# Two key tiles as one unit of seven block products, the last tile's quarters stored one by one, and a new written order

## The chip, the core and the metric

The kernel runs on one core of a Trainium2 chip. A core has five engines that run their own instruction streams: TensorE (PE in the profile) multiplies matrices, VectorE (DVE) and ScalarE (ACT) do elementwise work, GpSimd (POOL) does small elementwise work and issues DMAs, SyncE (SP) issues DMAs. The operands lie in the on-chip memory SBUF; matrix products arrive in PSUM, which has eight banks. The engines wait for each other and for DMAs by semaphores.

The metric is device time in microseconds (us) of one execution; the kernel before takes 203.65 us, median of 3 runs (203.56 to 203.76).

## The reference, cut to what matters

```python
xn = layernorm(A_x)                          # [2048, 640]
q, k, v = split(xn @ wqkv)                   # 32 heads of 20
pq, pk = phi(q), phi(k)                      # phi(t) = (t + 1 if t > 0 else exp(t)) + 1e-6
kv = sum over s of pk[s]^T v[s]              # per head, 20 x 20
z  = sum over s of pk[s]                     # per head, 20
o  = (pq @ kv) / (pq . z + 1e-6)
s  = o @ wo
g  = silu(relu(xn @ w1) @ w2)                # w1 [640, 1728], w2 [1728, 640]
out = A_x + s * g                            # [2048, 640], bfloat16
```

Nothing of it is cut in either kernel. The 2048 rows are 16 tiles of 128 tokens; the 640 columns are five chunks of 128, or two halves of 320.

## The kernel before, in words

The kernel computes G = xn^T pk in place of v and kv (the v weights are multiplied into G later), folds kv and wo into one matrix wf, and so needs only the products with wq, wk, w1, w2, wf and G.

**Block products.** Most large products are done with the seven-product scheme (Strassen's, in Winograd's form): a 2 x 2 block product takes seven block products for eight, at the price of sums of the operands on VectorE before it and of additions of results after it. One such set is called a unit. Its steps are s1, s5, s6, s2, s7, s3, s4, each a group of matmuls into one PSUM bank with what evacuates it. Of the five chunks of 128 in the inner dimension, four go into the scheme and the fifth is added by plain matmuls, so that a unit of width 512 has 2, 2, 2, 3, 3, 3, 3 matmuls in this order (`unit`, line 1164 on; its matmuls have line 1198, its copies on ScalarE line 1205, the additions on VectorE line 970, where the helper `tt` stands). The units are named by a letter and a number:

- a and b: hidden layer, relu(xn w1), tokens 0 to 1023 (a) and 1024 to 2047 (b). p and q: the query product, the same two halves of the tokens. m: the fifth column block of the query product with the last block of the hidden layer.
- g: G, eight matmuls of 320 columns per step. u: the product with w2, seven matmuls of 320 columns per step. o: the product with wf, steps of 2, 2, 2, 3, 3, 3, 3 matmuls of 320 columns.
- k: two key tiles, 8+i and 12+i, in one unit of 320 columns (`k_unit`). The kernel before has its code but does not use it.

**Other steps in the order.** n8 to n15 take the statistics of a token tile (for 9 to 15), normalise it on VectorE (line 649) and transpose it by a DMA on SyncE (line 698). H and Q are plain blocks of five 512-column matmuls, hh the narrow last hidden block. Ka9 and Kb9 are the two halves of the key product of tile 9, five 320-column matmuls each (line 709), with exp and relu on ScalarE (line 1482); the second half lets VectorE form pk (lines 735, 737). T0 and T1 are the sums of xn that the units of the two token halves need: five VectorE operations, of which T1's read the transposed tiles 8 to 15. SQ, SH1, SH2, SM, SK are the sums of weights for the units of q, h, m and k. y0 to y15 add pk tile by tile into two running sums for z, by accumulating DMAs that GpSimd issues (line 897), y0 to y7 into one and y8 to y15 into the other; each waits for the one before on its sum. zm merges the first sum into the second, zs splits the result into a high and a low part (lines 910, 970), zc makes the column z (line 916), dn the denominators (line 929). The two running sums lie in the hidden layer's buffer, in places that the units b4 and b5 write later; those writes wait until the sums are read. c0 and c1 are the last row block of G. GS and GT are sums for g, uT, uSa, uSb, oT, oS those for u and o. do, rc, dv store the reciprocals of the denominators, load them spread out, and multiply them into the queries. kv0, kv1 and W0 to W5 (lines 1595, 1621) make wf, the results going to their place by DMAs. xa, xb, xc load x tiles 10-11, 12-13, 14-15; wa and wb load parts of w1, w2a to w2d parts of w2; wo, wv0, wv1 the other weights; rb brings the row scales in by a transposing DMA; mv6 builds a small mask on GpSimd. e0, e1, e3 and f0, f1, f3 are halves of the last two token tiles, product with wf (e) and gating, addition of x and store (f); l0 and l1 are the two quarters of the last tile's first half (`s_last`), 160 columns each, five matmuls of 160 columns (line 1826).

**What sets the order.** The text PROGRAM (line 345) lists all steps after the head. TensorE and SyncE run exactly in this order. For ScalarE, VectorE and GpSimd a planner (`Sched.place`) orders the operations once, when the kernel is built, from estimated durations: it takes what can start first, and of several the one whose result is due first, among the next 60 operations. On the chip each engine runs its list in that order. The start of the kernel (layer norm of the first tiles, the key tiles 0 to 7, five hidden blocks) is written out before PROGRAM and is the head.

**The places of the key sums.** In the kernel before the sums of a k unit are laid out over the first running z sum and over wk itself:

```python
kSv = {i: two(regH[:, f * S + 1024:f * S + 1024 + 2 * HN], HN) for i, f in ((1, 4), (2, 10), (4, 3))}
kS3 = wk[:, 0:2, HN:D].bitcast(f16)
```

Of the kernel before, what the change touches and what calls it, by code (L numbers as in the profile page):

```python
# [346 lines left out]


def bass_recurrent_scan__linear_attn_block__dense_activation_relu__prompt_kernel(
# [135 lines left out]
    sumk = {9: [("hTs", 0, 5)], 5: [mSk[0], ("zacc", 1)], 11: [mSk[1], ("zacc", 1)], 4: [("zacc", 0)], 10: [("zacc", 0)]}  # L485
    hSk = [("hSs", u, i) for u in range(3) for i in (1, 2, 4)]
    NG = len(g_slots)
    mhalf = nc.alloc_sbuf_tensor("mhalf", [P, 1], f32)
# [416 lines left out]
        z_put(1, zacc[0], ("zacc", 0))  # L905

    def z_split():
        assert nz == [ZA, T + 1 - ZA - len(LATE)] and ("zacc", 1) not in dead, (nz, dead)
# [1 line left out]
        sc.op("ACT", lambda eng: eng.activation(out=hi, in_=zacc[1], func=ACTF.Copy), R=[("zacc", 1)],  # L910
              W=[("zhi",), ("ek_e", 0)])
# [737 lines left out]

    def gate_q(t, n, src, key):  # L1650
        g, sl = g_of(t)
        sc.op("ACT", lambda eng: eng.activation(out=g[:, HN * n:HN * (n + 1)], in_=src, func=ACTF.Silu),  # L1652
              R=[key, ("silu",)], W=[("g", sl, n)], extra=hz([("wv", 0), ("wv", 1)] + gtk))
# [296 lines left out]
```

## Time and profile before

| | |
|---|---|
| median of the runs | 203.65 us |
| profiled execution | 203.94 us |
| its span, first to last instruction | 202.7 us |
| TensorE busy | 198.6 us, 98% of the span, 1334 matmuls |
| VectorE busy | 172.2 us, 85% |
| ScalarE busy | 128.5 us, 63% |
| GpSimd busy | 37.2 us, 18% |
| granted TensorE clock | 1.000 |

A row of the groups reads: line, engine, operation, output <- inputs with shapes, count, then busy time and the mean of one in ns, then the engine's idle time before them and who ended it. A row of the timeline reads: start, duration, engine, line, operation, and in brackets the idle time just before it and what ended it; "xN" merges N neighbours. A row of the chain of waits reads: start, duration, what ran or was waited for. A row of the stretches reads: from:to, length, then busy time and instruction count of PE, weight loads, DVE, ACT and POOL, then clock, the DMA engines' share and GB/s. A row of waits reads: waiter <- releaser, total us, times, longest. Busy times count each engine's own overlaps once; matmul durations in the timeline are longer than the distance of their starts, since matmuls overlap.

### The profile page before, as it was taken

To read this page: it belongs to the slowest core of one execution; us is meant where nothing else is said; L and a number is where in the kernel's file an instruction comes from. 1 tells how busy PE (TensorE), PEld (TensorE's weight loads), DVE (VectorE), ACT (ScalarE), POOL (GpSimd) and SP (SyncE) were. 2 spreads that over 40 slices of the span, in tenths; PEclk is the share of its full clock that TensorE was granted. 3 is DMA by queue.
4 is the path that set the end of the run, shared out by engine and by line. 5 is a ranking of instruction groups with operands and counts; after the bars stand their busy time and mean duration, and the time that the engine had idled before them with its cause. 6 is when DMAs were issued, how large, how long until landed. Compare 5 with 4: busy or idle time off the path is not lost.

```text
span 202.7 us, 3677 instructions
## 1 busy us (share of the span) xinstructions
PE 198.6 (98%) x1334; PEld 123.8 (61%) x1344; DVE 172.2 (85%) x404; ACT 128.5 (63%) x268; POOL 37.2 (18%) x66
## 2 busy tenths in 40 slices
PE   8999999999999999999999999999999999999995
PEld 7755644545444454445645778777777777777773
DVE  4898999999997678899988879999978896855765
ACT  6497959799988486999662132463544645563452
POOL 3183051332256436422200000000000000000000
DMA  6976995662359858963462799338961106106103
GB/s 194 330 210 126 261 205 111 141 143 44 68 131 178 172 108 162 226 129 65 96 167 56 241 293 315 117 98 256 366 209 65 66 32 165 65 26 173 65 16 113
DMA packets 38328, 30.43 MB, mean 150 GB/s; under 512 B 13478, under 2 KB 38310, under 8 KB 38310
## 3 DMA queue, kind: packets, MB, share of 16 engines
q1 hardware_dynamic: 32437, 23.24, 41.0%
q0 software_dynamic: 4624, 5.57, 14.0%
q10 hardware_dynamic: 1248, 1.39, 2.1%
q8 instruction: 10, 0.16, 0.3%
q14 instruction: 9, 0.07, 0.1%
HBM read 15.81 MB, written 5.24 MB: 104 GB/s over the span
## 4 chain that ended last, share of the span: by engine, by line
PE 82%; DMA 11%; issue 3%; DVE 3%; ACT 0%; POOLq 0%; DVEq 0%
PE psT L1025 42%; PE psT L1198 18%; PE psT L709 10%; DMA regH<-reg 6%; PE psT L799 5%; DMA regH<-regH 3%; DMA reg<-in_A_x_dram 1%; PE psT L817 1%; PE psT L761 1%; PE psT L1826 1%; PE psT L682 1%; PE psT L1621 1%; PE psT L1595 1%; DVE regH L970 1%; PE psT L929 1%
## 5 line engine op out<-in xcount | busy, mean ns | idle before, releaser
L1198 PE MATMUL psT<-reg 128*128 128x512 bf16 (+1 forms) x135 | 36.8, 379 | 0.5 <-DVE regH L970 0.2
L1025 PE MATMUL psT<-reg,regH 128*128 128x320 bf16 (+1 forms) x224 | 35.0, 299 | 0.0
L1025 PE MATMUL psT<-reg 128*128 128x320 bf16 (+1 forms) x178 | 28.6, 299 | 0.0
L1025 PEld LDWEIGHTS psT<-reg,regH 128*128 128x128 bf16 (+1 forms) x224 | 21.9, 98 | 8.5
L1198 PEld LDWEIGHTS psT<-reg 128*128 128x128 bf16 (+1 forms) x141 | 13.4, 98 | 16.6 <-DVE regH L970 1.1
L897 POOL DMA_DIRECT2D regH<-reg x16 | 18.4, 1206 | 24.7 <-DMA regH<-reg 8.7
L1032 ACT ACTIVATE reg<-psT 128x320 f32<-128x320 f32 (+1 forms) x24 | 10.4, 435 | 17.8 <-PE psT L1025 15.9
L1025 PEld LDWEIGHTS psT<-reg 128*128 128x128 f16 (+1 forms) x178 | 17.4, 98 | 6.9
L970 DVE TENSOR_TENSOR reg<-reg 128x1024 f16<-128x1024 bf16 (+9 forms) x28 | 18.7, 673 | 1.1 <-PE psT L1025 1.0
L709 PE MATMUL psT<-reg 128*128 128x320 bf16 x120 | 18.7, 299 | 0.0
L1248 ACT ACTIVATE regH<-psT 128x512 bf16<-128x512 f32 (+1 forms) x24 | 15.2, 644 | 2.5 <-PE psT L1198 2.1
L1025 PE MATMUL psT<-reg,pqT 128*128 128x320 bf16 (+1 forms) x84 | 16.6, 299 | 0.0
L970 DVE TENSOR_TENSOR psT<-psT,reg 128x320 f32<-128x320 f32 (+1 forms) x21 | 11.4, 543 | 5.7 <-PE psT L1025 3.9
L1652 ACT ACTIVATE wv_sb<-psT 128x320 bf16<-128x320 f32 x22 | 9.6, 437 | 10.3 <-PE psT L1025 10.2
L709 PEld LDWEIGHTS psT<-reg 128*128 128x128 bf16 x120 | 11.7, 98 | 7.0
L1482 ACT ACTIVATE regE<-psT 128x320 bf16<-128x320 f32 x32 | 13.8, 538 | 2.9 <-PE psT L709 2.8
L630 DVE BATCH_NORM_STATS2 stats<-reg 128x6 f32<-128x320 bf16 x32 | 14.1, 473 | 1.3 <-DMA reg<-in_A_x_dram 1.3
L1032 ACT ACTIVATE psT<-psT 128x320 f32<-128x320 f32 x17 | 7.2, 426 | 10.3 <-PE psT L1025 10.3
L970 DVE TENSOR_TENSOR reg<-psT,reg 128x320 bf16<-128x320 f32 (+2 forms) x17 | 8.4, 499 | 4.2 <-PE psT L1025 4.1
L1841 ACT ACTIVATE reg<-psT 128x640 bf16<-128x640 f32 (+1 forms) x14 | 7.9, 569 | 5.1 <-PE psT L1025 5.1
L778 ACT ACTIVATE pqT<-psT 128x512 bf16<-128x512 f32 x16 | 10.6, 669 | 0.0
L776 ACT ACTIVATE regE<-psT 128x512 bf16<-128x512 f32 x16 | 10.1, 664 | 0.7 <-PE psT L761 0.5
(164 smaller groups left out, 385.5 us busy)
## 6 DMA issues: line engine op xcount, KB each, us to landing
regH<-reg POOLq DMA_DIRECT2D x16, 320.0 KB, 3.8
reg<-in_B_w_dram SPq DMA_DIRECT2D x12, 320.0 KB, 4.7
scr<-rden SPq DMA_DIRECT2D x4, 640.0 KB, 6.2
reg<-in_A_x_dram SPq DMA_DIRECT2D x4, 640.0 KB, 8.8
out_dram<-reg SPq DMA_DIRECT2D x14, 160.0 KB, 1.8
regE<-scr SPq DMA_DIRECT2D x3, 640.0 KB, 4.7
reg<-in_A_x_dram SPq DMA_DIRECT2D x4, 320.0 KB, 3.5
reg<-in_A_wo_dram SPq DMA_DIRECT2D x6, 160.0 KB, 5.2
```

The source lines that it names most:

```text
L630: sc.op("DVE", lambda eng: eng.bn_stats(stats[:, t, a, :], xv[:, HN * a:HN * (a + 1)]), R=[("xin", xs(t))], W=[("stats", t, a)])
L709: fns.append(lambda eng, a=a, k=k, lhs=lhs: eng.matmul(ps[bk[a]][:, 0:HN], lhsT=lhs, rhs=wk[:, k, HN * a:HN * (a + 1)], start=(k == 0), st ...
L776: exps.append(sc.op("ACT", lambda eng: eng.activation(out=e_, in_=src, func=ACTF.Exp), R=[key], W=[("er_e", es)]))
L778: sc.op("ACT", lambda eng: eng.activation(out=pqT[:, f, schunk(j)], in_=src, func=ACTF.Relu), R=[key], W=[("pqT", j, f)], extra=hz(gone))
L799: sc.group("PE", [(lambda eng, k=k: eng.matmul(ps[b], lhsT=w1_col(k, P * f, P), rhs=src[:, k, :], start=(k == 0), stop=(k == C - 1))) for ...
L897: dma("POOL", lambda eng: eng.dma_start(zacc[a], src, **kw), R=[key] + after, W=[("zacc", a)], chain=zchain[a])
L970: sc.op("DVE", lambda eng: eng.tensor_tensor(out=out, in0=in0, in1=in1, op=op), R=R, W=W, extra=extra)
L1025: sc.group("PE", [(lambda eng, k=k, lhs=lhs, rhs=rhs: eng.matmul(ps[b][:, 0:HN], lhsT=lhs, rhs=rhs, start=(start and k == 0), stop=(k == n ...
L1032: sc.op("ACT", lambda eng: eng.activation(out=dst, in_=ps[b][:, 0:HN], func=ACTF.Copy), R=[("ps", b)], W=[dkey], extra=extra)
L1198: sc.group("PE", [(lambda eng, k=k, lhs=lhs, rhs=rhs: eng.matmul(ps[b][:, 0:nn], lhsT=lhs if tile is None else rhs, rhs=rhs if tile is Non ...
L1248: sc.op("ACT", lambda eng: eng.activation(out=dst, in_=ps[b], func=ACTF.Relu), R=[("ps", b)], W=[("hT", j, f)], extra=ex)
L1482: sc.op("ACT", lambda eng, func=func, slot=slot: eng.activation(out=ek[:, eks(t), slot, HN * a:HN * (a + 1)], in_=ps[b][:, 0:HN], func=fun ...
```

## The change

1. The halves Ka9, Kb9, Ka13 and Kb13 leave the order; k1 (its seven steps) and SK come in. The sums of the k unit get other places, in the hidden layer's buffer at blocks 2, 3, 4 and 8, 9, 10, and the units b2, b3 and b4 wait to write there until k1 has read them. No sum lies over wk any longer.
2. The gate of the last tile's first half is done in two ScalarE operations of 160 columns. Each quarter is multiplied, added to x and stored by itself, l0's store on SyncE, l1's on ScalarE's queue; before, one addition and one store on ScalarE's queue served both.
3. The whole text PROGRAM is replaced by another order of the same other steps.

```diff
-xa T0 H14 SQ H112 n8 H15 H111 H110 xc n9 xb Q14 wb Q04 p1.s5 rb a1.s5 a1.s1 p1.s1 n11 Kb8 a1.s6 p1.s6 wa n10 p1.s2 SH1 a1.s2 a1.s7 n14 p1.s7 Ka9 a1.s3 a1.s4 n12 p1.s3 n15 p1.s4 p0.s1 Ka8 p0.s5 a0.s5 p0.s6 a0.s1 p0.s2 Kb11 a0.s6 p0.s7 p0.s3 n13 Ka10 Ka11 a0.s3 p0.s4 a0.s7 a0.s2 Kb9 Ka14 a3.s1 a0.s4 a2.s5 Kb12 a3.s5 a3.s6 a2.s1 hh0 hh1 y0 a2.s6 a3.s7 a2.s2 a3.s3 y1 a3.s2 a2.s7 a3.s4 T1 b1.s5
...
-q1.s6 y7 Kb15 m1.s1 y2 q1.s7 q1.s3 y6 m1.s5 q1.s4 y12 m1.s6 Ka15 m1.s2 m1.s7 b3.s1 b3.s5 m1.s3 b3.s6 w2a y13 m1.s4 b3.s2 b3.s3 SH2 b4.s1 b4.s5 y15 b3.s7 c0 b3.s4 c1 b5.s1 GT3 GS0 zm b4.s6 b5.s5 b4.s2 w2b b5.s6 b4.s7 zs GT1 b5.s2 w2d b4.s3 b4.s4 b5.s3 zc b5.s7 mv6 dn b5.s4 g0.s1
...
-g1.s4 uT3 uT2 do1 u0.s1 uSa0 kv1 kv0 u0.s5 u0.s6 sl W5
...
-e0 o6.s6 u7.s7 o6.s7 f0 o6.s3 e3 o6.s4 e1 u7.s3 u7.s4 l0 l1 f3 f1
+H111 H14 H15 xb H112 T0 H110 Q14 a0.s1 a0.s5 xa SQ n8 hh0 a0.s6 Q04 p1.s1 a0.s3 Kb8 rb a0.s7 p1.s5 a0.s2 p1.s6 a0.s4 p1.s2 a1.s5 a1.s1 n12 p1.s3 xc wa p1.s7 wb a1.s2 n11 a1.s6 Ka8 n13 SH1 p1.s4 SK a1.s3 n10 n15 p0.s5 mv6 n14 a1.s7 n9 p0.s1 Kb12 Ka12 a1.s4 p0.s6 a2.s5 a2.s1 p0.s2 p0.s3 a2.s6 p0.s7 a2.s2 T1 a2.s7 p0.s4 a2.s3 a2.s4 Kb11 b0.s1 k1.s1 k1.s5 Ka11 k1.s6 b0.s5 k1.s2 b0.s6 k1.s7 b0.s2 k1.s3 b0.s7 k1.s4 b0.s3
...
+Ka14 y2 y0 y14 b2.s7 y15 q1.s4 b2.s3 b2.s2 b2.s4 b3.s1 Ka10 GS0 GT1 GT2 b3.s5 w2a m1.s1 b3.s6 m1.s5 b3.s2 m1.s6 b3.s3 SH2 GT3 m1.s2 zm m1.s7 b3.s7 m1.s3 m1.s4 y10 zs b3.s4 c0 b4.s1 b5.s5 w2b b5.s1 w2d b4.s5 b4.s6 b4.s2 c1 b4.s7 b4.s3 b5.s6 b4.s4 g0.s5 g0.s1 b5.s3 b5.s2 b5.s7 zc g0.s6 b5.s4 g0.s2 dn g0.s3
...
+g1.s4 u0.s1 kv1 do1 kv0 W5 rc0 sl u0.s5
...
+uSb7 e1 u7.s7 o6.s4 e0 u7.s3 e3 f0 u7.s4 f1 f3 l0 l1
```

```diff
-    kSv = {i: two(regH[:, f * S + 1024:f * S + 1024 + 2 * HN], HN) for i, f in ((1, 4), (2, 10), (4, 3))}
-    kS3 = wk[:, 0:2, HN:D].bitcast(f16)
+    kSv = {i: regH[:, :].bitcast(f16).rearrange("p (f s) -> p f s", f=NK)[:, f:f + 7:6, o:o + HN]
+           for i, f, o in ((1, 4, 1024 + D), (2, 3, 1536), (4, 2, 1024), (3, 2, 1024 + HN))}
+    kS3 = kSv[3]
...
+    for i, f in ((1, 3), (2, 2)):
+        for f_ in (f, f + 6):
+            sumk[f_] = sumk.get(f_, []) + [kSk[i]] + [("kS3",)] * (f == 2)
...
-            tt(kS3, A11, A21, ALU.subtract, w, [("kS3",)], hz(w))
+            tt(kS3, A11, A21, ALU.subtract, w, [("kS3",)])
...
     def gate_q(t, n, src, key):
         g, sl = g_of(t)
-        sc.op("ACT", lambda eng: eng.activation(out=g[:, HN * n:HN * (n + 1)], in_=src, func=ACTF.Silu),
-              R=[key, ("silu",)], W=[("g", sl, n)], extra=hz([("wv", 0), ("wv", 1)] + gtk))
+        cuts = [(LC[i], LC[i + 1], ("g", sl, n) if i == 0 else ("glast",)) for i in range(2)] if t == LAST and not n else \
+            [(HN * n, HN * (n + 1), ("g", sl, n))]
+        for lo, hi, q in cuts:
+            sc.op("ACT", lambda eng, lo=lo, hi=hi: eng.activation(
+                out=g[:, lo:hi], in_=src[:, lo - HN * n:hi - HN * n], func=ACTF.Silu),
+                R=[key, ("silu",)], W=[q], extra=hz([("wv", 0), ("wv", 1)] + gtk))
...
-        tt(tmpo[:, NOUT, lo:hi], ps[b][:, 0:hi - lo], g[:, lo:hi], ALU.mult, [("ps", b), ("g", gslot[LAST], 0)],
-           [("tmpo", NOUT, 2 + i)])
-        if i:
-            s_store(LAST, NOUT, (2, 3), 0, HN, "DVE", "ACT")
+        tt(tmpo[:, NOUT, lo:hi], ps[b][:, 0:hi - lo], g[:, lo:hi], ALU.mult,
+           [("ps", b), ("glast",) if i else ("g", gslot[LAST], 0)], [("tmpo", NOUT, 2 + i)])
+        tt(outb[:, NOUT, lo:hi], tmpo[:, NOUT, lo:hi], xre[:, LAST, lo:hi], ALU.add,
+           [("tmpo", NOUT, 2 + i), ("xre", LAST // 4)], [("outb", NOUT, 2 + i)])
+        dma("ACT" if i else "SP", lambda eng: eng.dma_start(out2[tok(LAST), lo:hi], outb[:, NOUT, lo:hi]),
+            R=[("outb", NOUT, 2 + i)])
```

More of the change, by code (lines that the diff above doesn't have):

```diff
@@ new lines @@
+H111 H14 H15 xb H112 T0 H110 Q14 a0.s1 a0.s5 xa SQ n8 hh0 a0.s6 Q04 p1.s1 a0.s3 Kb8 rb a0.s7 p1.s5 a0.s2 p1.s6 a0.s4 p1.s2 a1.s5 a1.s1 n12 p1.s3 xc wa p1.s7 wb a1.s2 n11 a1.s6 Ka8 n13 SH1 p1.s4 SK a1.s3 n10 n15 p0.s5 mv6 n14 a1.s7 n9 p0.s1 Kb12 Ka12 a1.s4 p0.s6 a2.s5 a2.s1 p0.s2 p0.s3 a2.s6 p0.s7 a2.s2 T1 a2.s7 p0.s4 a2.s3 a2.s4 Kb11 b0.s1 k1.s1 k1.s5 Ka11 k1.s6 b0.s5 k1.s2 b0.s6 k1.s7 b0.s2 k1.s3 b0.s7 k1.s4 b0.s3 Kb14 a3.s5 a3.s1 b0.s4 Ka15 a3.s6 hh1 b1.s1 a3.s7 b1.s5 a3.s3 b1.s6 a3.s2 a3.s4 y8 b1.s2 q0.s5 q0.s1 b1.s7 Kb15 y12 y11 q0.s6 b1.s3 y7 b1.s4 q0.s2 ZS q0.s7 q0.s3 q1.s1 y9 y4 y3 y6 q0.s4 y1 q1.s5 q1.s6 b2.s5 Kb10 SM y5 b2.s1 q1.s2 y13 q1.s3 b2.s6 q1.s7 Ka14 y2 y0 y14 b2.s7 y15 q1.s4 b2.s3 b2.s2 b2.s4 b3.s1 Ka10 GS0 GT1 GT2 b3.s5 w2a m1.s1 b3.s6 m1.s5 b3.s2 m1.s6 b3.s3 SH2 GT3 m1.s2 zm m1.s7 b3.s7 m1.s3 m1.s4 y10 zs b3.s4 c0 b4.s1 b5.s5 w2b b5.s1 w2d b4.s5 b4.s6 b4.s2 c1 b4.s7 b4.s3 b5.s6 b4.s4 g0.s5 g0.s1 b5.s3 b5.s2 b5.s7 zc g0.s6 b5.s4 g0.s2 dn g0.s3 uSa0 g1.s1 GS1 w2c GT4 g0.s7 wo g1.s5 do0 g1.s6 g0.s4 uT3 wv0 g1.s7 g1.s2 uT1 g1.s3 uT2 wv1 g1.s4 u0.s1 kv1 do1 kv0 W5 rc0 sl u0.s5 W2 uSb0 W4 u0.s6 do2 uT4 u0.s2 W3 u0.s7 u0.s3 u2.s1 uSa2 W1 dv0 u2.s5 u0.s4 u2.s6 W0 uSa1 u2.s2 uSb2 rc1 u1.s1 uSa4 u1.s5 xre u1.s6 u1.s2 u2.s7 uSb1 u2.s3 oS0 uSb4 u1.s7 u1.s3 u2.s4 u1.s4 oT o0.s5 u4.s5 o0.s1 u4.s1 o0.s6 do3 o0.s2 u4.s6 o0.s3 o0.s7 rc2 u4.s7 o0.s4 uSa3 u4.s3 o1.s1 u4.s2 oS1 o1.s5 dv1 o1.s6 u4.s4 o1.s2 o1.s7 o2.s1 oS2 o2.s5 o1.s3 o1.s4 o2.s6 o2.s2 u3.s5 o2.s7 u3.s1 rc3 o2.s3 uSa6 uSb3 o2.s4 u3.s6 uSa5 o3.s1 oS3 u3.s2 o3.s5 o3.s6 u3.s7 dv2 u3.s3 oS4 o3.s7 o3.s2 u3.s4 u5.s5 u5.s1 uSb5 o3.s3 o3.s4 u5.s6 o4.s1 o4.s5 u5.s2 uSb6 o4.s6 u5.s7 u5.s3 oS5 o4.s2 o4.s7 u5.s4 o4.s3 o4.s4 u6.s1 o5.s1 o5.s5 u6.s5 uSa7 u6.s6 o5.s6 o5.s2 u6.s2 o5.s7 u6.s3 dv3 u6.s7 o5.s3 o5.s4 u6.s4 u7.s1 oS6 o6.s1 u7.s5 o6.s5 u7.s6 o6.s2 o6.s6 u7.s2 o6.s3 o6.s7 uSb7 e1 u7.s7 o6.s4 e0 u7.s3 e3 f0 u7.s4 f1 f3 l0 l1
@@ L907, in z_split @@
     def z_split():
-        assert nz == [ZA, T + 1 - ZA - len(LATE)] and ("zacc", 1) not in dead, (nz, dead)
+        assert nz == [ZA, T + 1 - ZA - len(LATE)] and ("zacc", 1) not in dead
         hi, lo = [v.rearrange("p (a n) -> p a n", a=2) for v in zhl]
@@ L1643, in bass_recurrent_scan__linear_attn_block__dense_activation_relu__prompt_kernel @@
     gslot = {}
+    LC = [0, 160, 320]
+    LAST = 15
     def g_of(t):
@@ L1806, in s_room @@
         return rooms[t]
-    LC = [0, 160, 320]
-    LAST = 15
     def s_mult(t, os_, i, lo, hi, src, keys, na):
```

3 lines of the change are left out of this document (1 added, 2 removed).

## The prediction

> **What bounds the kernel now.** I read the page first, then PE's waits, the chain of waits, and the timelines around the places that the new order moves.
>
> ```profile
> span 202.7 us, 3677 instructions
> ...
> PE 198.6 (98%) x1334; PEld 123.8 (61%) x1344; DVE 172.2 (85%) x404; ACT 128.5 (63%) x268; POOL 37.2 (18%) x66
> ...
> PE psT L1198 <- DVE regH L970: 0.2, 1, 0.2
> ...
> 49.77 1.36 PE psT L709 x10
> ...
> 41.04 2.37 PE psT L1198 x11
> ```
>
> TensorE (PE) is busy 98% of the span. Its list of waits holds, beside the start, one row, of 0.2 us. The chain's two rows give its pace: ten 320-column matmuls in 1.36 us are 0.136 us each, eleven 512-column ones in 2.37 us are 0.216. TensorE runs the written order as it stands, so I can place every step by counting matmuls from 23.30 us, where the order begins. Before the step b4.s4 stand 293 of 512 columns, 112 of 320 and the two hh steps (2.27 us in the chain): 104.05 by the count. The trace:
>
> ```profile
> 23.30 5.34 PE psT L799 x24
> ...
> 75.22 0.69 PE psT L709 x5
> ...
> 93.06 1.19 POOL L897 DMA_DIRECT2D regH<-reg  x1 [5.66 <-DVE regE L782]
> ...
> 97.48 1.19 POOL L897 DMA_DIRECT2D regH<-regH  x1 [3.23 <-DMA regH<-reg]
> ...
> 103.75 0.74 ACT L910 ACTIVATE regE<-regH 128x640 bf16<-128x640 f32 x1 [1.75 <-DMA regH<-regH]
> ...
> 103.82 0.69 DVE L970 TENSOR_TENSOR regH<-psT,wv_sb 128x512 bf16<-128x512 f32 x1 [0.62 <-PE psT L1198]
> ...
> 104.51 0.83 DVE L970 TENSOR_TENSOR regE<-regH,regE 128x640 bf16<-128x640 f32 x1
> ...
> 104.56 0.60 PE L1198 MATMUL psT<-reg 128*128 128x512 f16 x2 [0.18 <-DVE regH L970]
> ...
> 108.12 0.76 PE psT L1198 x3
> ...
> 134.50 0.27 PE psT L1621 x2
> ```
>
> Step Ka12 is counted to 75.18 and starts at 75.22: no time is lost until there. b4.s4 starts at 104.56, and W0 (count 133.69) at 134.50. So some 0.7 us are lost, nearly all between 100 and 109 us: 0.34 at b4.s4 (the matmul before it started at 104.00 and takes 0.216), 0.11 in the three matmuls at 108.12 (0.76 for 0.65), the rest in slivers at zc, b5.s7 and dn. The cause is in the rows: the merge of the two z sums (97.48) lands at about 103.72; only then may VectorE (DVE) write tile 10 of hT over the first sum (103.82), and only then is the PSUM bank free that b4.s4 wants.
>
> **Part 1: the unit.** Ka9, Kb9, Ka13 and Kb13 are 20 matmuls of 320 columns. k1 has 2+2+2+3+3+3+3 = 18. Gain 2 x 0.136 = **0.27 us** of TensorE. It costs, each at the nearest row:
>
> ```profile
> L970 DVE TENSOR_TENSOR reg<-reg 128x640 f16<-128x640 bf16 x3 | 1.4, 484 | 0.0
> ...
> L970 DVE TENSOR_TENSOR psT<-psT,reg 128x320 f32<-128x320 f32 x16 | 7.9, 496 | 4.1 <-PE psT L1025 3.9
> ...
> L1032 ACT ACTIVATE psT<-psT 128x320 f32<-128x320 f32 x17 | 7.2, 426 | 10.3 <-PE psT L1025 10.3
> ```
>
> VectorE: four weight sums (SK) at 0.48 and two additions from PSUM at 0.50, 2.9 us. ScalarE (ACT): two copies at 0.43, 0.86 us; exp and relu stay eight. Neither engine bounds the span, so this costs nothing where they have room. VectorE has none where it falls:
>
> ```profile
> 27.50:54.85 27.35, 27.19 (x148) 13.73 (x152) 26.64 (x76) 25.04 (x57) 6.71 (x17) 1.00 0.54 114
> ...
> 41.25 11.98 SPq L698 DMA_TRANSPOSE reg<-reg  x5
> ...
> 51.34 0.44 DVE L649 TENSOR_SCALAR reg<-reg,mv,rsy 128x640 bf16<-128x640 bf16 x1
> ...
> 54.88 0.68 DVE L970 TENSOR_TENSOR reg<-reg 128x1024 f16<-128x1024 bf16 x1
> ...
> 55.48 0.69 DVE L970 TENSOR_TENSOR psT<-psT,wv_sb 128x512 f32<-128x512 f32 x1
> ...
> 49.22 0.28 POOL L636 TENSOR_SCALAR rsv<-mv 128x1 f32<-128x1 f32 x1 [5.86 <-DVE mv L634]
> ...
> 54.90 1.69 POOL L897 DMA_DIRECT2D regH<-reg  x2 [3.80 <-DMA reg<-reg]
> ```
>
> In this stretch VectorE (fourth pair) works 26.64 of 27.35 us. The last of the tiles 8 to 15 is normalised at 51.34, its transpose is the last of the five at 41.25, and it lands at about 54.85: there T1, the five sums over these tiles, begins (54.88) and GpSimd (POOL) gets its first z sum. Before, their first reader was b1.s5, counted to 61.26: 6.4 us of room. After, b0.s1 (125 of 512, 25 of 320, one hh: 54.82) reads all eight tiles; k1.s5 (55.52) wants T1's first sum and SK's first; k1.s6 (56.47) three sums of T1 and two of SK. From T1's start that takes 3 x 0.60 (start to start: 54.88 to 55.48) + 2 x 0.41 (estimate: 0.48, less the 0.08 by which the sum of 54.88 overlaps the next) = 2.6 us. So TensorE waits unless T1 starts by 53.9, a microsecond sooner than now. Before T1 VectorE has two more evacuations (a2.s6, a2.s7, 0.6 each) and one K tile less (0.7): +0.5. It can put off what nobody awaits, four sums of p0 and one K tile, some 2 us; the new order asks for all norms by 45 us, so these go first. I take T1 at 54.1 and a wait of **0.2 us**. Ends: 0 (these sums put off) and 1.5 (T1 at 55.4, nothing put off). SyncE (SP) carries the same 7 transposes, 3 x loads, rb, wa and wb, in another order: xc, wa and wb now stand behind n12's transpose, so behind VectorE's norm of tile 12. SH1, which needs wa and wb, feeds a2.s5 at 47.66; with n12 at 35 us there are ten microseconds for it, so 0. mv6's six small POOL operations move from 106 to 44 us into POOL's waits for VectorE (5.86 us before the row at 49.22): 0; without that cover six at that row's 0.28, 1.7 us, on the norms' way.
>
> **Part 2: the z chain.** The last K half is Ka10 (86.2) for Ka15 (87.4), and zc moves from 105.3 to 107.9. The order on this chain is now y14, y15, merge, y10, split. By the rows a step takes 4.42 us (93.06 to 97.48), a merge 6.25 (to 103.73), a split 1.6. With y14 issued at X, the merge lands at X+15.1 and the split is done at X+21.1. b4.s4, counted to 103.13, can start if the merge lands by 102.4; zc if the split is done by 108.1. Both give X up to about 87.2.
>
> ```profile
> 61.50:80.00 18.50, 18.39 (x94) 9.12 (x94) 13.93 (x31) 13.38 (x28) 8.61 (x9) 1.00 0.77 150
> ...
> 80.00:97.00 17.00, 16.95 (x88) 8.46 (x88) 15.66 (x37) 16.93 (x36) 5.65 (x5) 1.00 0.63 139
> ...
> 91.24 0.88 ACT L1482 ACTIVATE regE<-psT 128x320 bf16<-128x320 f32 x2
> ...
> 92.28 0.48 DVE L737 TENSOR_TENSOR reg<-regE 128x640 bf16<-128x640 bf16 x1
> ```
>
> Ka14's matmuls end at 82.6 by the count. Before, Ka15's ended at 88.1 and its z sum went out at 93.06, 5.0 later: ScalarE evacuated it only at 91.24 and VectorE finished at 92.7. ScalarE (fifth pair) has room until 80 us and none from 80 to 97; Ka15 came 7.4 us into that full stretch. Ka14 comes at 81.9, and the q and m steps that fill ScalarE (ten and seven activations each) stand wider apart around it, so its backlog should be smaller. Without any, evacuation and finish take 0.88 + 0.9 us, about 1.8; with the old one 5.0. Nearer the old, since q1 still runs there, I take 4.2 us, X = 86.8, and the **0.55 us** of waits between 100 and 109 go. Ends: all 0.7 go; or 0.6 stay, with X = 87.6 or more.
>
> **Part 3: from 110 us on.** The same steps in another order. VectorE's reciprocals come 4.7 us later with dn (110.9); do0 then is behind wo on SyncE, and the divided q is first wanted at o0, 146 us: covered. The one spot with no cover is W5, which before stood two u steps after kv0 and now follows it at once:
>
> ```profile
> 125.04 1.44 PE psT L1595 x30
> ...
> 126.15 0.95 DVE L970 TENSOR_TENSOR reg<-psT,mv 128x40 bf16<-128x40 f32 x3
> ...
> 128.22 0.71 PE L1621 MATMUL psT<-reg 128*128 128x320 bf16 x4
> ```
>
> kv1's half of these matmuls (0.72 of 1.44) must be evacuated by two of the three DVE operations (0.6 together) while kv0's 0.72 run: a wait of 0 if VectorE is free, 0.6 if it is in a sum of 0.62. I take **0.2**.
>
> **Part 4: the tail.**
>
> ```profile
> 199.40 0.85 PE L1826 MATMUL psT<-reg,pqT 128*128 128x160 bf16 x10
> ...
> 199.60 0.44 ACT L1652 ACTIVATE wv_sb<-psT 128x320 bf16<-128x320 f32 x1 [0.51 <-PE psT L1025]
> ...
> 200.06 0.55 DVE L970 TENSOR_TENSOR reg<-psT,wv_sb 128x160 bf16<-128x160 f32 x2 [0.27 <-ACT wv_sb L1652]
> ...
> 200.65 0.33 DVE L1819 TENSOR_TENSOR reg<-reg 128x320 bf16<-128x320 bf16 x1
> ...
> 201.01 0.37 ACTq L1822 DMA_DIRECT2D out_dram<-reg  x1
> ...
> L1841 ACT ACTIVATE reg<-psT 128x640 bf16<-128x640 f32 x7 | 4.9, 701 | 4.4 <-PE psT L1025 4.4
> ...
> L1819 DVE TENSOR_TENSOR reg<-reg 128x640 bf16<-128x640 bf16 x14 | 6.7, 486 | 0.1
> ...
> out_dram<-reg ACTq DMA_DIRECT2D x1, 80.0 KB, 1.6
> ```
>
> From the gate's start to the last store's issue it is 1.41 us. After: first half gate 0.31 (estimate: 320 columns take 0.44, 640 take 0.70), product 0.32; second product about 0.67 to 0.99, when its matmuls too are done (200.25, 0.65 after the gate); sum of 160 columns 0.25 (estimate from 0.33 for 320 and 0.49 for 640): issue at 1.28 if VectorE takes both products first, 1.44 if sum 0 goes between. One store more, on SyncE, which has the f stores behind it. Gain **0.13**, ends 0.25 and -0.05.
>
> The rule against it: the Trainium skill ("DMA: Bandwidth & Descriptors", Specifications) puts 512 B as the least transfer for full rate, with a read-modify-write below. The quarters' rows are 320 B, the half's 640 B. By that rule the last store would land later, not sooner; the time is in the third rival.
>
> **Sum.** -0.27 - 0.55 - 0.13 + 0.2 + 0.2 = -0.55 us. The profiled execution took 203.94 us (span 202.7 and 1.2 around it), 0.29 above the median of 203.65. Against it the sum gives 203.4, against the median **203.1**.
>
> **The rivals.**
> 1. VectorE is late at 55 us (slower). For: 26.64 of 27.35 us are taken already, and 6.4 us of room become none. Against: some 2 us of it can wait. Each 0.1 us by which T1 starts after 53.9 is 0.1 us of TensorE; the sum without this wait is -0.75, so it decides for slower (over +0.4) from T1 at about 55.05, 0.2 later than now. With T1 at 55.4 to 56.2: 204.4 to 205.2.
> 2. The z chain is as late as before, pk14 5.0 us or more after Ka14. For: the merge and two steps more stand behind y14. Against: Ka14 meets ScalarE earlier in its full stretch. Then 0.6 us stay: 203.7.
> 3. The quarters don't shorten the tail, because their stores land later. For: a smaller store gains little, 1.6 us for 80 KB. Against: half the bytes. If the 40 KB land 0.2 us later than the 80 KB did, the tail gains nothing and loses 0.1: 203.3.
>
> **How the numbers follow.** 0.2%, 0.41 us, is about what a measurement of this kernel can tell from no change. My forecast (waits at 100 to 109 gone, little new) 0.47, all but a little of it below 203.24; rival 1 0.26; rival 2 0.20; rival 3 0.07. Faster 0.46, same 0.28, slower 0.26. The forecast's own range is 202.6 (no new wait, every old one gone) to 203.3. The range reaches into rival 1 as far as 204.5: below and above it I leave 0.2.
>
> **What would show it.** The K halves' matmuls fall by 20, and the units' line gains 18 of 320 columns. Around 55 us: the start of T1 (the first 1024-column f16 sum after the last transpose) and any gap before k1.s6. At 100 to 109: the regH<-regH merge against b4.s4. At 125: the gap before the first L1621. At the end: two 160-column sums and two 40 KB stores, issue to span end. The prediction is wrong if T1 starts after 55, or if a stretch that I called covered (SyncE's order at 30 to 45 us, the reciprocals at 112 to 117) shows waits of TensorE.

## The result and the profile after

The kernel after takes 203.28 us (median; 202.88 to 203.87), the kernel before 203.81 us beside it (203.41 to 204.16). The ratio is 0.9973 with a 95% interval of 0.9965 to 0.9980: 0.55 us less, between 0.41 and 0.71. The forecast was 0.55 less and 203.1 us. The total came out, but most of its terms did not, and they made up for each other; that the total is so close is luck. The profiled execution of after took 202.95 us, its span is 201.7 us. Lines of the kernel text stand four further down than before up to about line 1640 and eight or nine behind that: the units' matmuls are on L1202 for L1198, those of g, u and o on L1029 for L1025, the sums on L974 for L970.

The head of the page of after:

```profile
span 201.7 us, 3704 instructions
...
PE 198.4 (98%) x1342; PEld 122.7 (61%) x1342; DVE 172.9 (86%) x411; ACT 129.1 (64%) x271; POOL 37.9 (19%) x66
```

TensorE is as full as before. Its list of waits has one row left, the start of the kernel; the row of 0.2 us for a sum of VectorE is gone:

```profile
PE psT L602 <- PEq L1945: 0.8, 1, 0.8
```

The chain of waits is now TensorE alone from 4.48 us to the tail. Two of its rows (start, duration, what ran), at the place where the head ends:

```profile
17.35 5.43 PE psT L713 x40
22.78 5.40 PE psT L803 x25
```

and the same place before:

```profile
17.81 5.43 PE psT L709 x40
23.25 0.05 issue
```

The head, the part ahead of the new order and the same in both kernels, ends at 22.78 us with its last 320-column matmul; before it ended at 23.25. So 0.47 of the 0.99 us between the two profiled executions is not the change. It arises at the start. The timeline of TensorE before, and the same matmuls after:

```profile
5.38 0.74 PE L709 MATMUL psT<-reg,regX 128*128 128x320 bf16 x2
```

```profile
5.38 0.45 PE L713 MATMUL psT<-reg,regX 128*128 128x320 bf16 x2
```

Two matmuls of 320 columns took 0.74 us once and 0.45 the other time, without a wait. Over all profiled executions of this study the head ended between 22.61 and 23.93 us. I therefore set the two traces side by side from the end of the head: 179.43 us before (202.68 - 23.25), 178.94 after (201.72 - 22.78), a difference of **-0.49 us**, which agrees with the medians. Times given below as "from the head" are counted so. (The 23.30 from which the prediction counts is the start of the second matmul of the order: before shows 24 matmuls in that piece where after shows 25, so the record of the first, some 0.22 us earlier, is missing.)

**Around 55 us.** The timeline of after, rows of VectorE, GpSimd and TensorE:

```profile
47.95 0.80 DVE L653 TENSOR_SCALAR reg<-reg,mv,rsy 128x640 bf16<-128x640 bf16 x2
...
52.94 1.69 POOL L901 DMA_DIRECT2D regH<-reg  x2 [5.07 <-DMA reg<-reg]
...
53.02 1.29 DVE L974 TENSOR_TENSOR reg<-reg 128x1024 f16<-128x1024 bf16 x2
...
54.62 0.69 DVE L974 TENSOR_TENSOR reg<-reg 128x1024 f16<-128x1024 f16 x1
...
56.11 0.43 PE L1202 MATMUL psT<-regH,reg 128*128 128x320 f16 x2
```

The last norm, the second of the two at 47.95, starts at 48.3, 3.0 us sooner than before (51.34). The last transpose has landed by 52.9 (GpSimd, which waited for it, starts its z sums at 52.94), and T1 starts at 53.02: 30.2 us from the head, where I had taken 30.85 (54.1 - 23.25) and needed 30.65. The last sum that k1.s6 reads, T1's third, ends at 55.31 (54.62 + 0.69), and k1.s6 starts at 56.11 with no wait in its row: 0.8 us to spare.

**The z chain.** The timeline of after, and the merge's row of the DMA issues:

```profile
81.76 0.84 PE L713 MATMUL psT<-reg 128*128 128x320 bf16 x5
...
85.43 2.41 POOL L901 DMA_DIRECT2D regH<-reg  x2 [3.98 <-DVE regE L786]
89.38 1.19 POOL L901 DMA_DIRECT2D regH<-reg  x1 [1.53 <-DMA regH<-reg]
93.27 1.19 POOL L901 DMA_DIRECT2D regH<-regH  x1 [2.71 <-DMA regH<-reg]
99.08 1.19 POOL L901 DMA_DIRECT2D regH<-reg  x1 [4.62 <-DMA regH<-regH]
...
103.00 0.59 PE L1202 MATMUL psT<-reg 128*128 128x512 f16 x2
```

```profile
regH<-regH POOLq DMA_DIRECT2D x1, 320.0 KB, 5.5
```

Ka14's matmuls (81.76) are followed by y14's issue at 85.43. A step takes 3.9 us (89.38 to 93.27) for the 4.42 of before; the merge lands 5.5 us after its issue, at 98.8, and GpSimd issues y10 behind it at 99.08. b4.s4 (103.00) starts without a wait, 4.2 us behind the merge; before, it started 0.84 behind it.

**W5.** The last row of kv and the first of W5:

```profile
123.95 1.60 PE L1599 MATMUL psT<-reg,wv_sb 128*128 128x120 bf16 x30
125.39 0.43 PE L1625 MATMUL psT<-reg 128*128 128x320 bf16 x2
```

30 matmuls in 1.44 us, then W5 directly: no wait.

**The tail.** The timeline of after:

```profile
198.48 0.85 PE L1834 MATMUL psT<-reg,pqT 128*128 128x160 bf16 x10
...
198.68 0.50 ACT L1661 ACTIVATE wv_sb<-psT 128x160 bf16<-128x160 f32 x2 [0.51 <-PE psT L1029]
199.09 0.67 DVE L974 TENSOR_TENSOR reg<-psT,wv_sb 128x160 bf16<-128x160 f32 x2 [0.21 <-PE psT L1834]
199.68 0.38 DVE L974 TENSOR_TENSOR reg<-reg 128x160 bf16<-128x160 bf16 x2
199.94 0.33 SPq L1877 DMA_DIRECT2D out_dram<-reg  x1
200.10 0.37 ACTq L1877 DMA_DIRECT2D out_dram<-reg  x1
```

From the gate's start to the last issue it is 1.42 us (198.68 to 200.10), before 1.41. The first product starts 0.41 after the gate, not 0.31: it waited for TensorE (0.21), since l0's own matmuls were not done. Behind it stand four operations of VectorE where three stood, and the shorter gate is used up.

**Small losses.** The rest is slivers that no list of waits shows, found by following the count of matmuls step by step. In the new order, the timeline of after around hh0 and around a2.s1 (with ScalarE):

```profile
29.52 0.59 PE L1202 MATMUL psT<-regE,pqT 128*128 128x512 f16 x2
30.05 1.26 PE L821 MATMUL psT<-reg 128*32 128x512 bf16 x20
31.24 0.61 PE L1202 MATMUL psT<-regX,pqT 128*128 128x512 f16 x2
...
45.66 1.52 ACT L1486 ACTIVATE regE<-psT 128x320 bf16<-128x320 f32 x4
46.92 0.75 ACT L1252 ACTIVATE regH<-psT 128x512 f16<-128x512 f32 x1
...
47.14 0.59 PE L1202 MATMUL psT<-regE 128*128 128x512 f16 x2
47.72 1.25 PE L1202 MATMUL psT<-reg 128*128 128x512 bf16 x5
```

Two 512-column matmuls are 0.43 us from start to start; at 29.52 the next began after 0.53, at 47.14 after 0.58. The first is the change to 32-column weights (0.09; with the change back 0.19 a step). The second is a2.s1, which waited 0.15 for a bank that ScalarE emptied only at 46.92 to 47.67, behind the four operations of key tile 12. One more of 0.05 stands at b2.s6. Before had slivers of its own, shown here with the weight loads (PEld), whose rows name what held them:

```profile
77.70 0.59 PE L1198 MATMUL psT<-reg,pqT 128*128 128x512 f16 x2
78.26 0.11 PEld L1198 LDWEIGHTS psT<-reg 128*128 128x128 bf16 x2 [0.46 <-DVE regH L970]
...
90.64 0.38 PE L1198 MATMUL psT<-reg 128*128 128x512 bf16 x1
91.01 0.11 PEld L1198 LDWEIGHTS psT<-reg,rden 128*128 128x128 f16 x2 [0.48 <-ACT psT L1205]
```

The matmuls behind these loads start at 78.27 (b0.s4) and 91.01 (b3.s6): 0.57 for two matmuls (0.13 lost) and 0.37 for one of 0.216 (0.15 lost). The first waited for an addition of VectorE, the second for a copy of ScalarE, neither for z. These 0.28 us are gone in after as well; the prediction had put them between 100 and 109 us. What it read there as slivers at dn, two of 0.09, is the change to 32-column weights and back (at 106.55 and 107.74 before), and after has it too (at 110.70 and 111.81).

### The profile page after: what moved, and what is told of

Same layout as the page of the kernel before. It is cut to its first block, busy times and chain, and to the rows that moved or that the text cites. A ratio compares the mean times of both kernels' runs of the same rounds, so it can differ in the third digit from the quotient of the medians.

```text
span 201.7 us, 3704 instructions
## 1 busy us (share of the span) xinstructions
PE 198.4 (98%) x1342; PEld 122.7 (61%) x1342; DVE 172.9 (86%) x411; ACT 129.1 (64%) x271; POOL 37.9 (19%) x66
## 4 chain that ended last, share of the span: by engine, by line
PE 96%; DMA 1%; DVE 1%; issue 0%; DVEq 0%
PE psT L1029 42%; PE psT L1202 30%; PE psT L713 9%; PE psT L803 5%; PE psT L1500 2%; DMA reg<-in_A_x_dram 1%; PE psT L1834 1%; PE psT L821 1%; PE psT L765 1%; PE psT L1625 1%; PE psT L686 1%; PE psT L1599 1%; PE psT L933 1%; DVE reg L974 0%; DVE stats L634 0%; DVE reg L679 0%
## 5 line engine op out<-in xcount | busy, mean ns | idle before, releaser
L1202 PE MATMUL psT<-reg 128*128 128x512 bf16 (+2 forms) x150 | 39.8, 374 | 0.0
L1029 PE MATMUL psT<-reg,regH 128*128 128x320 bf16 (+1 forms) x224 | 35.0, 299 | 0.0
L1029 PE MATMUL psT<-reg 128*128 128x320 bf16 (+1 forms) x178 | 29.2, 299 | 0.0
L1029 PEld LDWEIGHTS psT<-reg,regH 128*128 128x128 bf16 (+1 forms) x224 | 21.8, 98 | 8.6
L1202 PEld LDWEIGHTS psT<-reg 128*128 128x128 bf16 (+1 forms) x150 | 14.3, 98 | 16.8 <-DVE regH L974 0.8
L1029 PEld LDWEIGHTS psT<-reg 128*128 128x128 f16 (+1 forms) x178 | 17.3, 98 | 7.4 <-issue 0.4
L974 DVE TENSOR_TENSOR reg<-reg 128x1024 f16<-128x1024 bf16 (+10 forms) x30 | 19.0, 649 | 0.1
L1661 ACT ACTIVATE wv_sb<-psT 128x320 bf16<-128x320 f32 (+1 forms) x23 | 9.6, 423 | 14.0 <-PE psT L1029 13.7
L974 DVE TENSOR_TENSOR psT<-psT,reg 128x320 f32<-128x320 f32 (+1 forms) x21 | 11.4, 545 | 5.4 <-PE psT L1029 5.1
L713 PE MATMUL psT<-reg 128*128 128x320 bf16 x100 | 15.5, 299 | 0.0
L1029 PE MATMUL psT<-reg,pqT 128*128 128x320 bf16 (+1 forms) x84 | 15.3, 299 | 0.0
L974 DVE TENSOR_TENSOR reg<-psT,reg 128x320 bf16<-128x320 f32 (+2 forms) x17 | 8.5, 502 | 5.9 <-PE psT L1029 5.9
L713 PEld LDWEIGHTS psT<-reg 128*128 128x128 bf16 x100 | 9.8, 98 | 5.6
L1486 ACT ACTIVATE regE<-psT 128x320 bf16<-128x320 f32 x24 | 10.5, 514 | 0.6 <-PE psT L713 0.6
L642 POOL TENSOR_TENSOR rsy<-rsv,mhalf 128x1 f32<-128x1 f32 x16 | 10.1, 635 | 1.1
```

The source lines that it names most:

```text
L642: sc.op("POOL", lambda eng: eng.tensor_tensor(out=rsy[:, t:t + 1], in0=rsv[:, t:t + 1], in1=mhalf[:, :], op=ALU.pow), R=[("rsv", t), ("mha ...
L713: fns.append(lambda eng, a=a, k=k, lhs=lhs: eng.matmul(ps[bk[a]][:, 0:HN], lhsT=lhs, rhs=wk[:, k, HN * a:HN * (a + 1)], start=(k == 0), st ...
L974: sc.op("DVE", lambda eng: eng.tensor_tensor(out=out, in0=in0, in1=in1, op=op), R=R, W=W, extra=extra)
L1029: sc.group("PE", [(lambda eng, k=k, lhs=lhs, rhs=rhs: eng.matmul(ps[b][:, 0:HN], lhsT=lhs, rhs=rhs, start=(start and k == 0), stop=(k == n ...
L1202: sc.group("PE", [(lambda eng, k=k, lhs=lhs, rhs=rhs: eng.matmul(ps[b][:, 0:nn], lhsT=lhs if tile is None else rhs, rhs=rhs if tile is Non ...
L1486: sc.op("ACT", lambda eng, func=func, slot=slot: eng.activation(out=ek[:, eks(t), slot, HN * a:HN * (a + 1)], in_=ps[b][:, 0:HN], func=fun ...
```

## The experiments

Ratios are to the kernel before, run on the same chip beside each; "over after" is the difference of the ratios (after's is 0.9973) times 203.8 us.

**The merge of the z sums, sooner and later.** First in the kernel before, alone:

```diff
- y15 b3.s7 c0 b3.s4 c1 b5.s1 GT3 GS0 zm b4.s6
+ zm y15 b3.s7 c0 b3.s4 c1 b5.s1 GT3 GS0 b4.s6
```

> The kernel before with one word moved: the merge of the two z sums comes ahead of y15 in the order, not after it, so that it no longer waits for the last key tile. Theory (the waits of 0.55 to 0.7 us between 100 and 109 us come from the merge landing at 103.7): the merge is issued some 3 us earlier, b4.s4 follows the matmul before it at once, and the time falls by 0.4 to 0.7 us against the kernel before. Rival (those slivers come from VectorE and the PSUM banks themselves, the merge only happened to land then): the time stays within 0.15 us.

203.48 us, ratio 0.9991 [0.9978, 1.0004]: 0.2 less by the ratio, 0.33 by the medians, and the interval reaches past no change. The 0.4 to 0.7 that I expected did not come. In the trace the merge goes out at 90.89 for 97.48 and b4.s4 no longer waits, but Ka9, long before, lost 0.37 us. TensorE's waits beside the start:

```profile
PE psT L709 <- DMA reg<-in_A_wqkv_dram: 0.4, 1, 0.4
PE psT L709 <- DMA reg<-reg: 0.2, 1, 0.2
```

The second row is Ka9 (37 us) waiting for tile 9's transpose; the first lies in the head. So the wait at b4.s4 is shown to come from the merge. Its 0.35 us were won there, and in the profiled execution given away in another place. Then the opposite, in the kernel after:

```diff
- m1.s2 zm m1.s7 b3.s7 m1.s3 m1.s4 y10 zs b3.s4
+ m1.s2 m1.s7 b3.s7 m1.s3 m1.s4 y10 zm zs b3.s4
```

> The changed kernel with the merge moved behind y10, so that it waits for the last key tile as it did before. Theory (a merge that lands after about 102 us holds b4.s4 up): y10 goes out at 93.3, the merge at about 97.6, and lands at 103 to 103.7; b4.s4 waits 0.5 to 1.0 us, and the time is 0.4 to 1.0 us above the changed kernel. Rival (the merge's place in the chain does not matter, since the split ends at the same time): the same within 0.15 us.

204.75 us, ratio 1.005 [1.0032, 1.0068], 1.6 over after. TensorE's waits:

```profile
PE psT L1202 <- DVE regH L974: 1.4, 1, 1.4
```

The merge went out 5.2 us later from the head (98.95 - 23.25 against 93.27 - 22.78). It took 4.3 us to land here, 5.5 in after, so it landed 4.0 later, and b4.s4 lost 1.55 by the count. So some 2.5 us of cover had stood between the landing and b4.s4 in after. The chain is what I said it was, with a larger price than I gave.

**The unit against plain halves.** First with the four halves in the places of k1's steps:

```diff
- p1.s4 SK a1.s3
+ p1.s4 a1.s3
...
- b0.s1 k1.s1 k1.s5 Ka11 k1.s6 b0.s5 k1.s2 b0.s6 k1.s7 b0.s2 k1.s3 b0.s7 k1.s4 b0.s3
+ b0.s1 Ka9 Ka11 Kb9 b0.s5 b0.s6 Ka13 b0.s2 b0.s7 Kb13 b0.s3
```

> The changed kernel without the unit: Ka9, Kb9, Ka13, Kb13 stand at the places of k1's steps, SK is gone; all else of the new order stays. Theory (the unit is worth its two matmuls, its sums are hidden): 0.27 us slower than the changed kernel, some 203.5 against a before of 203.8. Rival (VectorE's 2.9 us more make slivers of waits between 45 and 62 us, which eat the gain): no slower than the changed kernel, or faster.

204.63 us, ratio 1.0042 [1.0025, 1.0059], 1.4 over after instead of 0.27. The timeline, ScalarE and TensorE:

```profile
56.42 2.15 ACT L1486 ACTIVATE regE<-psT 128x320 bf16<-128x320 f32 x6
...
57.97 1.04 PE L1202 MATMUL psT<-reg,pqT 128*128 128x512 f16 x4 [0.39 <-ACT regE L1486]
```

Three halves in a row give ScalarE six operations in a row, and b0.s5 waits for its bank. I spread the halves out:

```diff
- Kb11 b0.s1 k1.s1 k1.s5 Ka11 k1.s6 b0.s5 k1.s2 b0.s6 k1.s7 b0.s2 k1.s3 b0.s7 k1.s4 b0.s3 Kb14 a3.s5
+ Kb11 b0.s1 Ka9 Ka11 b0.s5 b0.s6 b0.s2 b0.s7 Kb9 b0.s3 Kb14 a3.s5
...
- a3.s6 hh1 b1.s1 a3.s7 b1.s5 a3.s3 b1.s6 a3.s2 a3.s4 y8
+ a3.s6 hh1 b1.s1 a3.s7 Ka13 b1.s5 a3.s3 b1.s6 a3.s2 a3.s4 Kb13 y8
```

> The kernel after without the unit k1 and its weight sums; Ka9 directly behind b0.s1, Kb9 behind b0.s7, Ka13 in a3 and Kb13 behind a3.s4, so that no two of the four halves stand together. Theory (the unit is worth its two matmuls, and the 1.35 us that the plain halves cost in e2_plain_halves were 0.27 of matmuls and some 0.9 of waits because ScalarE had four halves to evacuate at once): 0.27 us over the kernel after, 203.55, and no row of TensorE waits over 0.2 us between 55 and 62 us. Rival A (the unit spares more than TensorE, so plain halves cost wherever they stand): 0.6 us or more over the kernel after, with waits of TensorE again. Rival B (the two matmuls are not seen at all): level with it.

207.2 us, ratio 1.0155 [1.0133, 1.0177], 3.7 over after. My theory fell here: the waits became longer, not shorter. Two of them in the timeline:

```profile
57.30 1.04 PE L1202 MATMUL psT<-reg,pqT 128*128 128x512 f16 x4 [1.07 <-ACT regE L1486]
...
59.74 0.82 PE L1202 MATMUL psT<-reg 128*128 128x512 f16 x3 [0.75 <-DVE psT L974]
```

The first stands behind three halves close together again (Kb11, then behind b0.s1 Ka9 and Ka11). The second is b0.s7 waiting for VectorE; nothing stands between b0's steps s6, s2 and s7 any more, so, as I read it, k1's matmuls there had also been the time in which b0's banks were emptied. Neither run measures what the unit is worth, because each changes the spacing. So I kept the order and gave k1 its two matmuls back:

```diff
+            ks = list(enumerate(l_))
+            if start and tile is not None:
+                ks = ks[0:1] + ks
...
-                for k, (lhs, rhs) in enumerate(l_)], R=R + xall + ([] if start else [("ps", b)]), W=[("ps", b)])
+                for k, (lhs, rhs) in ks], R=R + xall + ([] if start else [("ps", b)]), W=[("ps", b)])
```

> The kernel after, but in k1.s1 and k1.s5 the first matmul is issued twice (both write the bank from the start, so the second overwrites the first): k1 has 20 matmuls, as many as the four plain halves, in the same order and with the same sums. Theory (TensorE sets the pace there, so the unit is worth its two matmuls): 0.27 us over the kernel after, 203.55, the same waits. Rival (the two matmuls only eat time in which TensorE would have waited for VectorE's sums): level with it.

203.86 us, ratio 1.0004 [0.9995, 1.0013], 0.6 over after, more than the 0.27. But the spans differ by 0.3 only (202.3 us in the median against 202.0), and from the head by 0.34 (202.19 - 22.92 = 179.27 against 178.94). The other 0.3 lie outside the span: this kernel's runs have 1.55 to 1.64 us around the span, those of every other kernel 1.19 to 1.31. Why, no run shows. The two matmuls cost their 0.27 us, within what the spans resolve.

**VectorE's room at 55 us.** Four and eight sums of 640 columns ahead of SK, which change no result:

```diff
+    def k_more():
+        sc.allow_unread.add(kSk[0])
+        tt(kSv[1], wk[:, 0:2, HN:D], wk[:, 2:4, HN:D], ALU.add, [("wk", q) for q in range(C)], [kSk[0]])
...
-        "SK": lambda: run([(k_S, i) for i in (1, 3, 2, 4)]),
+        "SK": lambda: run([(k_more,)] * 4 + [(k_S, i) for i in (1, 3, 2, 4)]),
```

> The kernel after with four more sums of 640 columns on VectorE ahead of SK (work added, nothing else changed): 4 x 0.41 = 1.6 us more of VectorE before T1. Theory (VectorE has 0.8 us between T1's third sum and k1.s6, and some 2 us of it before T1 can be put off, which the planner does): 0 to 0.4 us over the kernel after, T1 at 53.0 to 54.2. Rival 1 (VectorE has no room at 55 us; what is added before T1 moves T1 by as much): 0.8 us over it, T1 at 54.6.

> The same with eight sums: 3.3 us more of VectorE before T1. Theory: with 0.8 us of room and about 2 us that can be put off, 0.5 to 1.2 us over the kernel after, T1 at 54.3 to 55. Rival 1 (each microsecond beyond the 0.8 is a microsecond of TensorE): 2.5 us over it, T1 at 56.3.

204.25 and 205.72 us; ratios 1.0007 [0.9992, 1.0022] and 1.0080 [1.0061, 1.0099], 0.7 and 2.2 over after; by the count of matmuls 0.87 and 2.35 us at b0.s1, k1.s5 and k1.s6. The waits with eight sums:

```profile
PE psT L1202 <- DVE regH L974: 1.2, 2, 0.8
...
PE psT L1202 <- ACT regE L780: 0.5, 1, 0.5
```

1.6 us of work cost 0.87, 3.3 us cost 2.35: in both all but some 0.8 to 0.95 us. The rival had the price (0.8 and 2.5), my theory did not. But T1, by which both were to be told apart, went another way. It starts at 54.12 and 55.37, from the head 0.27 and 2.3 us later than in after; on after's clock that is 53.3 and 55.4, where the theory had 53.0 to 54.2 and 54.3 to 55, the rival 54.6 and 56.3. With four sums the timeline shows what k1.s6 waited for instead:

```profile
57.26 0.48 DVE L974 TENSOR_TENSOR regH<-regH,reg 128x640 f16<-128x640 f16 x1
...
57.80 0.45 PE L1202 MATMUL psT<-regH,reg 128*128 128x320 f16 x2 [0.42 <-DVE regH L974]
```

It is the second of SK's sums, which stand behind the added ones; it ends at 57.74. VectorE does put T1 ahead of some of the added work; what k1 needs as a whole comes later by as much as was added. The room at k1.s6 is 0.8 us, and beyond it a microsecond of VectorE is about a microsecond of the kernel.

**The tail as before, in the kernel after.**

```diff
-        cuts = [(LC[i], LC[i + 1], ("g", sl, n) if i == 0 else ("glast",)) for i in range(2)] if t == LAST and not n else \
+        cuts = [(LC[i], LC[i + 1], ("g", sl, n) if i == 0 else ("glast",)) for i in range(2)] if False else \
...
+        if i:
+            s_store(LAST, NOUT, (2, 3), 0, HN, "DVE", "ACT")
```

> The changed kernel with the old end: one gate of 320 columns, two products, one sum, one store on ScalarE's queue. By the prediction's term it is 0.13 us slower than the changed kernel. By the trace of the changed kernel, where the last store is issued 1.42 us after the gate's start as against 1.41 before, the time is the same within 0.1 us. Rival (the short rows' store lands later): the old end is faster, by 0.1 us or more.

203.30 us, ratio 0.9973 [0.9958, 0.9988]: the same as after. From the gate's start to the last issue it is 1.42 us here too:

```profile
198.90 0.44 ACT L1661 ACTIVATE wv_sb<-psT 128x320 bf16<-128x320 f32 x1 [0.51 <-PE psT L1029]
...
200.32 0.37 ACTq L1830 DMA_DIRECT2D out_dram<-reg  x1
```

**A second unit**, for the key tiles 10 and 14, in the kernel after:

```diff
- b0.s3 Kb14 a3.s5 / b2.s5 Kb10 SM / q1.s7 Ka14 y2 / b3.s1 Ka10 GS0
+ b0.s3 a3.s5 / b2.s5 SM / q1.s7 y2 / b3.s1 GS0
...
- b1.s4 q0.s2 ZS q0.s7 q0.s3 q1.s1 y9 y4 y3 y6 q0.s4 y1 q1.s5 q1.s6 b2.s5
+ b1.s4 k2.s1 q0.s2 k2.s5 ZS q0.s7 k2.s6 q0.s3 k2.s2 y9 y4 y3 y6 k2.s7 q0.s4 y1 k2.s3 b2.s5
...
- y5 b2.s1 q1.s2 y13
+ y5 k2.s4 b2.s1 q1.s1 q1.s5 q1.s6 q1.s2 y13
```

> The kernel after with the key tiles 10 and 14 as a second unit k2, its steps between b1.s4 and b2.s1, in place of Ka10, Kb10, Ka14 and Kb14. Theory (a unit is worth its two matmuls where VectorE and ScalarE have room; in the stretch 61.5 to 80 VectorE worked 13.9 of 18.5 us, ScalarE 13.4): 0.27 us under the kernel after, 203.0, no new row in TensorE's waits. Rival 1 (the two additions of results and the later evacuations find VectorE taken, as forecast for k1 at 55 us): 0.2 to 0.8 us over it, with a wait of TensorE in k2 or b2. Rival 2 (the z chain now ends later, since tile 14 lies in another place): a wait at b4.s4, as in the kernel before, 0.2 over it.

208.03 us, ratio 1.0201 [1.0177, 1.0226], 4.6 over after. Rival 1's mechanism, but far beyond its price; three steps of q1 moved behind k2 as well, and the run does not part that from the unit. From the timeline, the first of some ten places:

```profile
75.65 1.09 PE L1202 MATMUL psT<-reg 128*128 128x320 bf16 x5 [0.85 <-DVE regH L1255]
```

That VectorE worked 13.9 of 18.5 us in this stretch said nothing on whether the bank wanted next was empty.

**Two moves against the small losses.** hh0 beside hh1, so that the weights change their width once:

```diff
- n8 hh0 a0.s6 / Kb11 b0.s1 k1.s1 / a3.s6 hh1 b1.s1
+ n8 a0.s6 / Kb11 hh0 hh1 b0.s1 k1.s1 / a3.s6 b1.s1
```

> The kernel after with hh0 moved from a0 and hh1 from a3 to one place, between Kb11 and b0.s1. Theory (of the small losses, 0.16 us lies in each change between 128- and 32-column weights, twice for separate hh steps, once for adjacent ones): 0.16 us under the kernel after, 203.1. Rival (the steps from 30 to 53 us come 1.2 us sooner than VectorE and the transposes can follow): TensorE waits between 40 and 55 us, 0.3 to 1.2 us over it.

206.5 us, ratio 1.0134 [1.0119, 1.0149], 3.3 over after. The waits begin where hh0 was taken away:

```profile
30.84 0.59 PE L1202 MATMUL psT<-regX,pqT 128*128 128x512 f16 x2 [0.40 <-ACT psT L1209]
...
35.44 0.61 PE L1202 MATMUL psT<-regE,pqT 128*128 128x512 f16 x2 [0.74 <-ACT regE L1486]
```

hh0's 1.19 us had been the time in which ScalarE copied a0's first results; the second wait is ScalarE again, at p1.s5. The rival had waits, but between 40 and 55 us, and at most 1.2 us over after. And Ka12 two steps later:

```diff
- Kb12 Ka12 a1.s4 p0.s6 a2.s5
+ Kb12 a1.s4 p0.s6 Ka12 a2.s5
```

> The kernel after with Ka12 two steps later, behind p0.s6, so that ScalarE does not evacuate both halves of key tile 12 in a row (1.52 us) ahead of the bank that a2.s1 needs. Theory: a2.s1's 0.17 us goes, 0.1 to 0.17 under the kernel after. Rival (as in the other moves, another bank comes late in its place): 0.1 to 0.5 over it.

203.01 us, ratio 0.9966 [0.9954, 0.9978], 0.14 under after, which the times alone do not tell from it; it is clearly faster than before. From the head the spans differ by 0.17 (201.75 - 22.98 = 178.77 against 178.94), about what a2.s1 had lost. The timeline shows the step that I aimed at:

```profile
46.50 0.71 ACT L1252 ACTIVATE regH<-psT 128x512 f16<-128x512 f32 x1
...
47.34 0.59 PE L1202 MATMUL psT<-regE 128*128 128x512 f16 x2
47.77 1.24 PE L1202 MATMUL psT<-reg 128*128 128x512 bf16 x5
```

a2.s1 starts 0.43 after a2.s5: the wait is gone. It is the lowest median of the kernels here.

## Why the prediction came out

| term of the sum | forecast | measured |
|---|---|---|
| two matmuls of the unit | -0.27 | -0.3 (span of the run with both put back) |
| waits before, at 100 to 109 us | -0.55 | -0.35 (b4.s4 alone) |
| waits before, at 78 and 91 us | in the row above | -0.28 |
| tail | -0.13 | 0 |
| T1 and SK late at 55 us | +0.2 | 0 |
| W5 directly behind kv0 | +0.2 | 0 |
| small losses of the new order | 0 | +0.39 (0.19 each at hh0 and hh1, 0.15 at a2.s1, 0.05 at b2.s6, less 0.19 that the adjacent hh steps lost before) |
| sum | -0.55 | -0.49 from the head |

The measured terms add up to -0.54, and to -0.51 with the unit at its 0.27: they account for the -0.49 within what the count of single steps resolves.

- **The unit.** Right for its two matmuls, in size and in reason. What the unit as a whole is worth against four halves that are well placed was not measured. That VectorE does the added work for nothing held with 0.8 us to spare, no more.
- **The z chain.** Right in reason: the merge sets b4.s4, shown from both sides. Sizes were off to the safe side: y14 went out 62.7 us from the head (85.43 - 22.78), forecast 63.5, because ScalarE took Ka14 sooner than I allowed, and a step took 3.9 for 4.42, the merge 5.5 for 6.25. The step that failed is "nearly all between 100 and 109 us": of what before lost, z held up 0.35, at b4.s4; 0.28 lay at 78 and 91 us and had nothing to do with z, and the slivers at dn were no waits and did not go. The count hid this, because it began at 23.30, 0.2 us behind the order's first matmul.
- **T1.** The step that failed is T1 at 54.1, by way of what VectorE puts off. The size was wrong: T1 came 0.6 sooner from the head. The reason holds in part: key tile 12, which ScalarE had evacuated by 47.2 (the four operations at 45.66), got its VectorE work only from 57.36 on, behind T1. In both traces T1 starts just behind the landing of the last transpose (54.85 and 54.88 before, 52.9 and 53.02 after), and the last norm came 3.0 us sooner; but VectorE works without a pause in the two microseconds before T1 in both, so whether the landing or VectorE's own work set it is not shown. Rival 1's mechanism, a late VectorE, is there, as the added sums show, 0.8 us beyond where this kernel stands. Its sign was not: the sums of SK were late, more than T1.
- **The tail.** The step that failed is the product at 0.31: it awaits l0's matmuls as well as its gate. Rival 3's result (no gain) came, but not by its way. Both store sizes took the same from issue to landing, as this row of after's DMA issues shows against the 1.6 us of the prediction's row for 80 KB:

```profile
out_dram<-reg ACTq DMA_DIRECT2D x1, 40.0 KB, 1.6
```

  The rule of the Trainium skill ("DMA: Bandwidth & Descriptors", Specifications) on transfers under 512 B would, as the prediction drew on it, have made the 320 B rows land later. They landed no later, 1.6 against 1.6 us; whether they would have landed sooner without it, no run here shows.
- **W5.** No wait came; the low end was right.
- **What was not in the sum** is the fault that weighs most: I counted a new order as the moved terms alone and priced the spots that I had looked at. 0.39 us of slivers stand in spots that I had not, and 0.2 of the waits at 100 to 109 us and the tail's 0.13 were not won; two costs of 0.2 that did not come and the 0.28 at 78 and 91 us made up for them. That is luck, not a sum that held.

What stays open: why the four moves of steps cost as much as 1.4 to 4.6 us; their first waits are shown, what each passed on to the next was not followed.
